# One fused attention and wave-MLP kernel, its steps written out in another order

## The chip, the core and the metric

The kernel runs on one of the eight cores of a Trainium2 chip. A core has four compute engines, each with its own queue of instructions: TensorE (PE; its weight loads are listed apart, as PEld), VectorE (DVE), ScalarE (ACT) and GpSimd (POOL). SyncE (SP) has a queue too and issues nearly all DMA transfers. The engines run side by side, and wait for each other through semaphores. The metric is the device time of one execution in microseconds (us), lower is better.

## The reference

Eight batches; in each, an attention over 8 heads of 576 tokens with 64 channels, and behind it a small token-and-channel network on 576 x 512 values. The attention is the sum of two: one over q, k and v averaged in fours (144 tokens, every output repeated four times), and one in which a token sees only the tokens less than 4 away.

```python
q_d, k_d, v_d = (t.reshape(B, H, Sd, 4, D).mean(axis=3) for t in (q, k, v))
out_up = np.repeat(sm_attn(q_d, k_d, v_d), 4, axis=2)
mask = np.abs(pos[:, None] - pos[None, :]) < 4
scores = np.where(mask, scale * q @ k^T, -1e9)
out_local = softmax(scores) @ v
x = (out_up + out_local) as [batch, token, 512]

theta = x @ w_theta
zr, zi = x * cos(theta), x * sin(theta)
y = w_tok_r @ zr + w_tok_i @ zi          # mixes tokens
u = x + y
out = u + relu(u @ w_ch)
```

Inputs and output are float32.

## The kernel before, in words

All compute runs in bfloat16 with float32 sums. The work of a batch is cut into steps of one function each, named by two letters; one step issues some instructions on one engine. The order is not left to a scheduler: the string `ORDER` names every step of the whole kernel in one row, 1,191 words, and `pin()` chains each instruction to the one before it on its engine, so every queue (SyncE's too) is in exactly the order of the words. A word is the step's two letters and a place; which batch and which part of it is meant follows from counting (the third `mx` is the third in the list of `STEPS`). The place is a PSUM bank or a pair of banks for steps on PE, a staging slot for loads, and the engine (`v`, `a`, `g` for DVE, ACT, POOL) for casts, copies and means.

The steps of a batch, in the order in which they need each other:

- `lk`, `lq`, `lv` and `lw` load k and q (four loads of 288 KB each) and v (ten of 128 KB: five windows, two halves) into one of 16 staging slots (L287, L347); v of batch 0 comes by `l1` (L365). A slot is free again when its cast has read it. `la`, `lb`, `lc` load the weights.
- `ck`, `cq`, `cv` cast to bfloat16 (L295, L396). `tp` transposes k or q on PE (L302), `ev` copies the result out of PSUM (L315); for batch 7 a DMA does it (`dk`, L306). `kd`, `qd` take the means of four (L321 on DVE, L329 to L335 on POOL).
- `ps`, `ex`, `mk`, `po`, `nm` are the local attention: scores (L482), exponential (L490), band mask (L503, L505), product with v (L515), division (L523, L524). `pv`, `vd`, `sd`, `ed`, `nd`, `xn`, `xd`, `xc` are the averaged one (L404 to L470).
- `xt` transposes the local result (L537) and `xa` adds the averaged one to it (L545): x, transposed, in `xT`.
- `th`, `cs` make theta and its cosine and sine (L556, L561, L562), `xm` transposes x back (L595), `zz` multiplies (L620, L615 for batches 6 and 7). `tt`, `ct`, `zt`, `zp`, `zc` or `dz` do the same for the last 64 tokens (L568 to L590).
- `mx` is the mixing of tokens: eight parts of nine matmuls with 288 columns (L636), each followed by `ua`, which adds x (L641). `wp`, `wc` transpose its weights once, in the beginning.
- `up`, `uc` or `du` transpose u (L650, L653, L645); `ch` projects it (L666), `rl` makes the output (L674), `st` stores it (L680). `ut`, `dt`, `ht`, `rt`, `ss`, `sr` do this for the last 64 tokens of two batches at a time (L656 to L709).
- `te` and `ts` let ACT load the table of the exponential or the sine ahead of its use (L770), and `wm` runs idle matmuls on zeros (L764). Six more idle matmuls belong to the constants (L226).

So a batch's q goes load, cast, transpose, copy, mean, and only then can its averaged scores (`sd`) start; its theta can start only when both attentions are through, its mixing only when all of its z is there. The order interleaves two or three batches, so that one batch's mixing fills PE while the next one's attention goes from engine to engine.

Of the kernel before, what the change touches and what calls it, by code (L numbers as in the profile page):

```python
# [58 lines left out]
lq8 x14 cka x15 cqg evv cva lk9 tp67 ckg cvv cva lqa lqb tp01 lk1 cqg x14 cva wm521 evv evv cqa qdv tp23 cva la3 eva
pv47 vda wm624 ps01 kdg la6 ps23 ex kdv ckg lq4 ex wm656 wm717 lq2 ps01 qdg lk5 sd67 mkv ckv cqg sd45 po23 ed lk8 cag  # L60
ed ex po67 lq9 lba nm cba nd45 nm nd23 xn cag mkg cqa tp01 po67 xn po45 nm lkb eva xd0 mkg ckg lq7 cka xca la1 po23 nm
tp67 cag xt45 la0 xt01 nm lb3 lb4 lb5 cqg lbc xa lba lb2 xt23 xa eva tp67 lb8 cqg lb1 caa ts th4 kdg cs cbg xm5 xa lv7
evv lw th0 th2 lv0 cbv lw zz cbg tt3 xm4 lv3 cs cbg cbv ct cbg cbg cs lvb lw lw wp0 wcv wp1 wcv ztg wp5 th3 wp1 lv8
wcv xm2 cbg xm0 zz zp7 tp45 cs qdg wp3 wp6 zz wcv lw zz wcv wcv zca eva wp7 wcv wp1 wca te wp0 wcv ps34 ps56 ex ex
ps12 mx0 lq1 cvg lk2 lka mx7 lqc mx3 qdv cvg ua lk7 ex ua lk0 mkv mkv kdg sd67 po45 nm sd12 lq4 cva lk5 lk9 cvg cvg ed
ed mx0 ua ua lq3 pv67 po45 po23 nm mx0 vda mkg nd67 lk8 nd45 lkb nm xn xn lq6 ckg ckg tp12 mx3 po45 ua lca ua nm cqg
cqg tp67 eva eva xd0 ckg ckg up1 lq7 po23 lvc xcv nm tp45 xt67 cqg mx0 cqg xt23 eva xt45 lv4 qdg kdg uca lw lv0 lw lw
lv3 lv1 lw lw xa xa tp67 cka ts ckg ckg th1 th2 xa th5 lk8 xm4 evv cs cqg xm1 ckv th3 zz tt4 up6 lq6 lqb cs zz tp12
xm7 ua cs ucv ct cs cqg eva te ztv xm6 zz zz mx0 ua tp34 zp7 tp56 ps12 zcv mx7 mx0 ex cvv kdg evv eva lk7 lk9 cvg lk4
qdg ua up7 uca sd12 mkv ps34 po56 ex ua ccv lcc lc5 kdg nm mkv mx0 sd34 ed po56 cvg cvg ua cqg mx7 nm ua ed mx0 ua lk2  # L70
cka cqg ps67 lqd lq0 cva po45 nm lca ex po23 ckg ckg nm pv01 lvb mx6 vda lk6 utv lw tp45 eva lv1 lw cca ccv nd01 nd23
ua xn xn qdg tp67 mx5 eva lv8 lv9 cqg cqg lw lw ccg ps34 qdg ps67 ua ps12 kdv ex ex xd0 lva xca lw mkg mkg lqc lq0 ch5
rl ckg ckg cvg cvg ch3 sd67 xt45 mkg ed rl ex ts mx0 xa xt67 po45 lv5 th1 cs xa nm ua tp23 th7 up4 up1 ucv xt56 xa mkv
lv4 ch0 eva po56 po23 cvg lq2 tt4 uca th1 cs th7 nm st nm xm2 lqb rl lq1 zz lqd ct cvg xm6 lw cqg ch5 cs zz cs cqa te
up0 up1 rl sd23 ucv po67 ch4 nm rl ch0 rl ucv tp67 lv7 ed cvg pv45 vdv lk8 lk9 eva st st tp23 eva xm0 ztg lk0 lka lw
xm1 zz zz zp7 ch6 zca lvc lv3 kdg nd45 xn nd23 ckg tp01 cva xn qdg utg mx7 cka ps23 rl kdg eva ps01 ua po45 mx6 up7 ex
ex lw lw lv8 nm qdg lw cqg po45 cqg ucv lvb lv2 lw sd23 sd01 lv5 ed mx7 lw lw ua tp23 nm xd4 ed ckg ckg xca st evv
tp01 eva mx6 mkg xt45 xt23 ua ua cva cvg cvg xt01 cka ts cvg xa xa mx7 th6 xa po45 nm pv23 tt0 th1 lk4 xm4 st st mkg
th5 vdv st cs nd23 ua zz ct cqg cqg ztg tp67 th4 cs dt po01 cs cs te xn evv po23 mx5 kdg qdg xm4 xm6 mx7 nm ps01 ex nm
ps23 ua lvd ua ex ch5 ps01 ex qdg zz lw lw xm7 zz rl kdg zp6 zz mkg nd23 xn lv1 lva lv3 mx5 zca sd67 lw ps01 ex po34  # L80
mx2 ua lw ed tp01 sd67 cva nm po34 eva cvv cvg ed lw up5 uca ua mx2 cvg nm cvg lvc xd3 ua pv04 xcv lk7 lk0 mx7 lq9 lq6
lq2 lqd lq8 lqb lq5 ckg ckg vda lq7 lw xt56 mkv cqg cqg po34 lk4 xt01 xa xa ch2 st cva ts lv6 th5 up6 ckg xm0 nm th1
tp34 cs ucv cs mkg rl eva mx6 ua ua th1 xt67 lk0 lk1 cs cqa po45 mkv xa nm ht3 rt tp67 th1 eva zz xm2 lv9 xm3 xm4 lw
lve zz zz ckg dk4 kdv mx0 cqg tp67 nd23 xn cs zz ua cqa eva mx1 nd67 xn cqa sr cqa cka tt2 ct dkb up4 cva cva ua mx0
mx7 ua cvg cvv uca te po01 nm qdg kdg qdg sd56 ed po23 ua ch4 rl xd0 ch1 ztg lw nm up7 ch4 uca xca po23 dz xt67 rl evg
ckg nm st st pv15 vda mx0 ps23 xa ex rl up1 up7 evg ua ucv mx6 uca ss ps01 ex xt45 cqa utg xa ua lv1 dk4 ps23 ex mx7
up0 uca th4 lvb sd56 mkv po23 lw lw xt01 utg dt ua dk7 cvv nm th7 du ed ts evg nd56 xa nd23 tt0 xn xn ct qdg mkv mkg
evv mx1 ztg xd2 up0 ua cs ch3 rl cs te mx4 ch7 qdg ps56 rl xcv ua mx1 ex cvg po23 po45 ua uca ps67 ex ht1 nm nm st st
rt cva ss mx0 ua po67 xt45 nm ps23 st xa ex ts du kdg th1 xm0 xm7 cs th6 cs xm4 zz zz zz ch5 rl kdg mx7 ua th0 po67 nm
cs te xt45 xa sd12 ch3 xm0 ch7 ch4 xt56 st ed sd12 mkg mkg ed ts zz dz lw mx0 lv1 du du cvv lw cvg th1 cs rl uta mx3  # L90
st rl rl xa dxb ua po45 po67 pv02 nm nm ua du mx1 vda ch4 dx mkg ua po23 po01 po67 rl sr nm mx5 ua mx4 tt5 dx1 du nm
nm nd23 xn nd01 st mx6 th7 mx2 cs xn xd3 mx0 ua ua xcv ua ua xt67 utv ct dx st st xt45 xt23 xa ch1 rl th0 ch6 ch1 ch7
cs xa xa tt0 zz zz th2 th3 cs st du du ch4 rl zz zz ztg ct dz rl mx2 mx0 mx1 cs ua ua st dxe dx ht0 ua th1 cs th3 dx7
dx zz st st mx2 rl mx1 ua ua cs zz dt mx3 mx1 mx2 zz zz ztg dz mx7 ua mx3 du du du mx6 rt ua ua utg ua st rl du st mx7
mx4 ua ua ua sr mx7 mx6 mx5 ua ua ua du du ua ch7 ch6 ss ch5 rl rl ch7 ch6 ch4 ch3 du du st uta dt sta rl st rl ht7
ch2 sta rl st rl sta rl st rt ssa sr rl sta rm su k0
"""


# [450 lines left out]


# [256 lines left out]
```

## Time and profile before

| | us |
|---|---|
| median of 3 runs | 231.89 |
| lowest, highest run | 229.57, 232.5 |
| span of the profiled execution | 232.2 |
| PE busy in it | 217.7 |
| DVE busy | 187.7 |
| ACT busy | 156.2 |
| POOL busy | 145.0 |

The profiled execution is one of its own beside the timed runs; of its time the profile has the span, from the first to the last instruction, and no other figure. A matmul's end is modelled in the profile and matmuls overlap, so a busy PE is not PE at its peak. The chain of waits is followed back from the last instruction: at each piece to what released it.

### The profile page before, as it was taken

To read this page: it belongs to the slowest core of one execution; us is meant where nothing else is said; L and a number is where in the kernel's file an instruction comes from. 1 tells how busy PE (TensorE), PEld (TensorE's weight loads), DVE (VectorE), ACT (ScalarE), POOL (GpSimd) and SP (SyncE) were. 2 spreads that over 40 slices of the span, in tenths; PEclk is the share of its full clock that TensorE was granted. 3 is DMA by queue.
4 is the path that set the end of the run, shared out by engine and by line. 5 is a ranking of instruction groups with operands and counts; after the bars stand their busy time and mean duration, and the time that the engine had idled before them with its cause. 6 is when DMAs were issued, how large, how long until landed. Compare 5 with 4: busy or idle time off the path is not lost.

```text
span 232.2 us, 9404 instructions
## 1 busy us (share of the span) xinstructions
PE 217.7 (94%) x3943; PEld 152.6 (66%) x3970; DVE 187.7 (81%) x367; ACT 156.2 (67%) x243; POOL 145.0 (62%) x192
## 2 busy tenths in 40 slices
PE   7997899999999999899999989989998999999992
PEld 3655678877877666776775675756655775668741
DVE  5699888999988799789968887698986978558473
ACT  4589799689988898898877978778788232430000
POOL 7689977879985999879963489598952001100000
PEclk9999799999999999999999999999999999999999
DMA  6999968997999689968999996892284358656587
GB/s 217 395 390 390 291 114 238 361 300 118 265 391 179 165 245 285 243 142 214 205 165 347 307 213 115 206 153 92 67 149 109 71 127 193 138 159 137 142 227 245
DMA packets 76795, 49.41 MB, mean 213 GB/s; under 512 B 61136, under 2 KB 61392, under 8 KB 76752
## 3 DMA queue, kind: packets, MB, share of 16 engines
q1 hardware_dynamic: 76096, 47.76, 81.9%
q10 hardware_dynamic: 656, 1.05, 1.3%
q8 instruction: 31, 0.51, 0.9%
q14 instruction: 12, 0.10, 0.1%
HBM read 33.98 MB, written 9.44 MB: 187 GB/s over the span
## 4 chain that ended last, share of the span: by engine, by line
PE 60%; DMA 10%; POOL 10%; issue 6%; ACT 5%; DVE 4%; SPq 4%; DVEq 0%; POOLq 0%; ACTq 0%
PE PS L636 21%; PE PS L666 9%; PE PS L556 8%; DMA st<-in_q_dram 6%; PE PS L302 4%; POOL two L329 3%; PE PS L515 2%; SPq L347 2%; DMA st<-in_k_dram 2%; PE PS L537 2%; DMA ur<-uT 2%; POOL q_tm L295 2%; PE PS L482 2%; PE PS L447 1%; PE PS L595 1%
## 5 line engine op out<-in xcount | busy, mean ns | idle before, releaser
L636 PE MATMUL PS<-WT,z 128*128 128x288 bf16 x576 | 78.0, 287 | 0.0
L636 PEld LDWEIGHTS <-z 128*128 128x128 bf16 x576 | 53.9, 98 | 15.9 <-issue 1.3
L641 DVE TENSOR_TENSOR uT<-PS,xT 128x288 bf16<-128x288 f32 x64 | 28.6, 452 | 12.7 <-PE PS L636 10.9
L561 ACT ACTIVATE cs<-PS,pihc 128x512 bf16<-128x512 f32 x32 | 22.0, 689 | 21.1 <-PE PS L556 13.4
L556 PE MATMUL PS<-wth,xT 128*128 128x512 bf16 x116 | 30.8, 383 | 0.7 <-issue 0.2
L666 PE MATMUL PS<-wch,uT 128*128 128x512 bf16 (+1 forms) x122 | 29.8, 373 | 0.9 <-issue 0.6
L524 DVE TENSOR_TENSOR tmp<-PS,rl 128x512 bf16<-128x512 f32 x40 | 27.7, 692 | 1.4
L545 DVE TENSOR_TENSOR xT<-PS,xdT 128x928 bf16<-128x928 f32 (+1 forms) x24 | 22.3, 952 | 3.7 <-PE PS L537 2.3
L674 DVE SCALAR_TENSOR_TENSOR osb<-PS,ur 128x512 f32<-128x512 f32 x28 | 19.1, 687 | 7.1 <-DMA ur<-uT 3.0
L490 ACT ACTIVATE pm<-PS 128x1024 bf16<-128x1024 f32 (+1 forms) x24 | 20.5, 880 | 6.2 <-PE PS L482 6.1
L577 POOL TENSOR_TENSOR zT<-xT,cst 128x512 bf16<-128x512 bf16 x7 | 9.7, 1383 | 20.6 <-ACT cst L574 20.6
L295 POOL CAST k_tm<-st 128x576 bf16<-128x576 f32 x23 | 15.1, 668 | 11.2 <-DMA st<-in_k_dram 11.1
L396 POOL CAST v_w<-st 128x512 bf16<-128x512 f32 x21 | 13.3, 651 | 10.6 <-DMA st<-in_v_dram 10.5
L770 ACT ACT_TABLE_LOAD x15 | 19.2, 1283 | 0.3
L666 PEld LDWEIGHTS <-uT 128*128 128x128 bf16 x132 | 11.9, 98 | 11.2
L562 ACT ACTIVATE cs<-PS 128x512 bf16<-128x512 f32 x32 | 19.1, 597 | 0.0
L556 PEld LDWEIGHTS <-xT 128*128 128x128 bf16 x128 | 11.7, 99 | 10.6 <-issue 0.6
L295 POOL CAST q_tm<-st 128x576 bf16<-128x576 f32 x23 | 15.4, 686 | 4.9 <-DMA st<-in_q_dram 4.7
L503 POOL TENSOR_TENSOR pm<-pm,band 128x512 bf16<-128x512 bf16 x16 | 18.3, 1164 | 0.0
L329 POOL TENSOR_TENSOR two<-qT 128x576 f32<-128x576 bf16 x14 | 16.5, 1177 | 0.7 <-ACT qT L315 0.4
L620 DVE TENSOR_TENSOR z<-PS,cs 128x1024 bf16<-128x1024 bf16 x24 | 15.8, 684 | 0.5 <-ACT cs L562 0.3
L437 ACT ACTIVATE pd<-PS 128x864 bf16<-128x864 f32 x16 | 13.8, 889 | 2.5 <-PE PS L426 2.5
(124 smaller groups left out, 422.9 us busy)
## 6 DMA issues: line engine op xcount, KB each, us to landing
st<-in_k_dram SPq DMA_DIRECT2D x32, 288.0 KB, 6.5
st<-in_q_dram SPq DMA_DIRECT2D x32, 288.0 KB, 6.3
...
```

Of the source, the lines that this page charges most:

```text
L295: COPY[w](out=to, in_=of)
L329: nc.gpsimd.tensor_tensor(out=t, in0=src[:, :, 0:2], in1=src[:, :, 2:4], op=ALU.add)
L490: nc.scalar.activation(out=pm[(3 * b + u) % NPM][:, :, 0:n].rearrange("p e c j w -> p e (c j w)"), in_=at.pop(("ps", b, u))[:, :, 0:4 * W ...
L524: nc.vector.tensor_tensor(out=tmp[(NCH * b + c) % NTMP].rearrange("p g (j d) -> p g j d", d=D), in0=ps[:, :, :, 0:D], in1=r.unsqueeze(3).t ...
L545: nc.vector.tensor_tensor(out=xT[b % 2][:, :, lo:lo + cnt].rearrange("p e (m j) -> p e m j", j=4), in0=at.pop(("xt", b, u))[:, :, 0:cnt].r ...
L556: nc.tensor.matmul(out=ps, lhsT=xT[b % 2][:, dc, P * c:P * c + P], rhs=wth[:, dc, :], start=(dc == 0), stop=(dc == 3))
L561: nc.scalar.activation(out=t[:, 0, :], in_=ps, func=AF.Sin, bias=pihc, scale=1.0)
L562: nc.scalar.activation(out=t[:, 1, :], in_=ps, func=AF.Sin, bias=0.0, scale=1.0)
L636: nc.tensor.matmul(out=ps, lhsT=z[b % 2][:, j, P * dc:P * dc + P], rhs=WT[:, j, cols], start=(j == 0), stop=(j == 8))
L641: nc.vector.tensor_tensor(out=uT[b % 2][:, dc, cols], in0=at.pop(("mx", b, i)), in1=xT[b % 2][:, dc, cols], op=ALU.add)
L666: nc.tensor.matmul(out=ps[:, cols], lhsT=uT[b % 2][:, dc, P * c:P * c + P], rhs=wch[:, dc, cols], start=(dc == 0), stop=(dc == 3))
L770: nc.scalar.activation(out=idle, in_=pihc, func=TABLE[kind])
```

## The change

Two things change. The first is `ORDER`: the same steps in a new row, again 1,191 words, with other banks, other slots and in part other engines. Nine more casts of k and q go to DVE (11 rather than 2), four fewer to ACT (12 rather than 16) and five fewer to POOL (41 rather than 46); three more of the `zt` go to DVE. The idle matmuls of `wm` are 25 with 10,560 columns, where they were 32 with 15,424. Table loads stay 16. The second is the code of `xt` and `xa`: the pair of banks may now be two that do not lie next to each other. What is multiplied and added, and with how many columns, stays.

```diff
 ORDER = """
-kcg l10 l11 l12 l13 kcv lk4 lq5 c1a wm7e0 kcg c1g t101 lk6 lk7 ckg c1a ckg c1v t123 e1a kcv e1v wm737 tp01 x12 cqa x13
...
+l10 lk1 ckv lk2 l13 c1a cka kcg c1v l14 l15 lq6 lq7 cqg lk0 wm087 tp01 t123 lk8 lq1 c1a evv kdv kcv c1a ckv cqg e1a
...
     def xt(b, u, w):
-        ps = at["xt", b, u] = pair(w).rearrange("p k (x n) -> p (k x) n", x=2)
+        ps = at["xt", b, u] = pair(w).rearrange("p k (x n) -> p k x n", x=2)
...
-                        nc.tensor.matmul(out=ps[W * (j % 2):W * (j % 2) + W, 2 * hf + j // 2,
+                        nc.tensor.matmul(out=ps[W * (j % 2):W * (j % 2) + W, hf, j // 2,
...
         nc.vector.tensor_tensor(
-            out=xT[b % 2][:, :, lo:lo + cnt].rearrange("p e (m j) -> p e m j", j=4),
-            in0=at.pop(("xt", b, u))[:, :, 0:cnt].rearrange("p e (m j) -> p e m j", j=4),
-            in1=xdT[b % 2][:, :, lo // 4:(lo + cnt) // 4].unsqueeze(3).to_broadcast([P, 4, cnt // 4, 4]),
+            out=xT[b % 2][:, :, lo:lo + cnt].rearrange("p (k x) (m j) -> p k x m j", k=2, j=4),
+            in0=at.pop(("xt", b, u))[:, :, :, 0:cnt].rearrange("p k x (m j) -> p k x m j", j=4),
+            in1=xdT[b % 2][:, :, lo // 4:(lo + cnt) // 4].rearrange("p (k x) m -> p k x m", k=2).unsqueeze(4)
+            .to_broadcast([P, 2, 2, cnt // 4, 4]),
             op=ALU.add)
```

The code grows by one line, so lines from L549 on are one higher in the changed kernel.

SyncE's queue around the loads of batch 6, before: the thirteen loads of v are of batches 4 and 5, the ten of batches 5 and 6, and the eight of q are batches 6 and 7. `st` is the staging area, `osb` an output buffer, `utr` the transposed last tokens.

```order
L347 DMA st_126<-in_v_dram 64x8x64 x13
L680 DMA out_0_dram<-osb3_121 128x512
L287 DMA st_126<-in_k_dram 128x576
L680 DMA out_0_dram<-osb4_122 128x512
L680 DMA out_0_dram<-osb0_118 128x512
L680 DMA out_0_dram<-osb1_119 128x512
L695 DMA_TRANSPOSE utr_117<-ut0_115 128x4x128
L347 DMA st_126<-in_v_dram 64x8x64 x10
L287 DMA st_126<-in_k_dram 128x576 x2
L287 DMA st_126<-in_q_dram 128x576 x8
```

And now: the seven loads of v are of batches 4 and 5, the four of q behind them are batch 6, the fifth is batch 7's first, and the three of k are batch 6.

```order
L347 DMA st_126<-in_v_dram 64x8x64 x7
L287 DMA st_126<-in_q_dram 128x576
L347 DMA st_126<-in_v_dram 64x8x64
L287 DMA st_126<-in_q_dram 128x576
L347 DMA st_126<-in_v_dram 64x8x64
L287 DMA st_126<-in_q_dram 128x576
L347 DMA st_126<-in_v_dram 64x8x64
L287 DMA st_126<-in_q_dram 128x576
L347 DMA st_126<-in_v_dram 64x8x64
L287 DMA st_126<-in_q_dram 128x576
L287 DMA st_126<-in_k_dram 128x576 x3
```

The q of batch 6 has moved ahead of sixteen loads of v and between the others; ahead of its first load there were 57 loads of v and 82 other issues, and there are now 41 and 71.

VectorE's queue in the start, behind the constants, before. `k_tm` and `q_tm` are casts of k and q, `kT` and `qT` their transposes, `kd` and `qd` the means, `z0` here holds v of batch 0, `pm` the exponentials.

```order
L371 CAST z0_103<-st_126 128x8x64
L371 CAST z0_103<-st_126 128x64
L231 COPY band_131<-full0_135 64x64 x2
L379 COPY xT1_102<-PS_61 128x1152
L315 COPY kT0_62<-PS_61 128x2x576
L393 CAST v_w0_70<-PS_61 128x8x64
L315 COPY qT0_64<-PS_61 128x1152
L315 COPY kT0_62<-PS_61 128x2x576
L321 TENSOR_REDUCE qd0_68<-qT0_64 128x288
L321 TENSOR_REDUCE kd0_66<-kT0_62 128x2x5x29
L505 TENSOR_TENSOR pm0_83<-pm0_83,band_131 128x1024
L295 CAST k_tm2_76<-st_126 128x9x64
```

And now:

```order
L295 CAST k_tm0_74<-st_126 128x9x64
L371 CAST z0_103<-st_126 128x8x64
L371 CAST z0_103<-st_126 128x64
L315 COPY kT0_62<-PS_61 128x2x576
L321 TENSOR_REDUCE kd0_66<-kT0_62 128x2x5x29
L231 COPY pu1_133<-full2_137 64x32 x2
L295 CAST k_tm1_75<-st_126 128x9x64 x2
L315 COPY kT0_62<-PS_61 128x2x576
L231 COPY band_131<-full0_135 64x64 x2
L295 CAST q_tm2_79<-st_126 128x9x64
L321 TENSOR_REDUCE qd0_68<-qT0_64 128x288
L393 CAST v_w0_70<-PS_61 128x8x64
```

Four casts of k and q stand there now where one stood, and the copies out of PSUM for q and for v's first transpose have gone to another engine.

More of the change, by code (lines that the diff above doesn't have):

```diff
@@ L57 @@
 ORDER = """
-kcg l10 l11 l12 l13 kcv lk4 lq5 c1a wm7e0 kcg c1g t101 lk6 lk7 ckg c1a ckg c1v t123 e1a kcv e1v wm737 tp01 x12 cqa x13
[L59 to L96, printed above, removed]
+l10 lk1 ckv lk2 l13 c1a cka kcg c1v l14 l15 lq6 lq7 cqg lk0 wm087 tp01 t123 lk8 lq1 c1a evv kdv kcv c1a ckv cqg e1a
@@ new lines @@
+wm422 t101 lq2 ckv cqg e1a wm431 tp23 x14 x15 tp01 eva x12 cqg cva kcg qdg lk9 lq3 x14 cva cva lk4 lk5 lq6 lk7 la0 lb8
+la1 la2 evv kcv cqv lba tp67 eva cva la3 lbb lbc wm341 ps01 x16 ex qdv cvv ps45 ckg kdg wm311 pv01 ckg ex ckg cqg cbg
+cag mkv vda cag sd45 po67 lb9 mkv po23 sd01 lq4 ed ed nm nm po67 lq5 lb6 tp45 lb0 nm eva nd23 xn lb1 ps01 nd67 xn tp45
+xt23 ex po01 eva xd6 xca nm lb8 xa cag cba lv2 ckg mkg wm711 xt45 po01 cbg cbg caa tp67 nm xa eva cbg th2 lw lv3 lw
+lv9 xt01 cqg wp3 wp6 cqg cbg lv6 lw kdg cbg cbg wcv cs wp7 wcv xa th4 wcv cbg tp56 tt0 xm7 ts cs lw lv8 xm1 wp2 th3
@@ new lines @@
+evv zz ct xm0 zz th7 xm1 cs ztv wcv lw zp6 wp3 cs ts wca zz wp2 wp5 wp0 ps47 zcv wcv zz wcv lk1 lk0 ps26 qdg ex wcv
+lq5 wp3 wcv kdv mx1 mx3 ua qdg cvg lq2 sd45 ex lk4 lqc lka ps07 ua mkv cvg mx1 ed ex po45 cva ua sd23 po67 nm nm cva
+mkg mx0 ed po45 cvg ckg mkg pv12 ckg cqg po67 te vda mx3 nd12 nm nd45 nm ua ua xn mx3 tp01 xn cqg xd2 ua xca eva po45
+xt67 cka nm mx3 xa tp45 xt01 xt67 th2 xa lv8 lq6 eva ua cs ckg cqg lq9 lk1 lk3 lk0 lw lv2 lq4 lva up4 xm5 lw tp01 ucv
+xa evv th3 lw lvc lk5 lcb lq7 tt4 cqg qdg ckg lv1 lw lw cqg cs ct tp67 xm2 th0 ztg ckg th3 cs zz evv mx6 xm7 up0 cs zz
@@ new lines @@
+zp1 kdv tp23 xm4 zca eva zz ua zz cqv kdg ps57 mx6 ex mx1 tp23 cvg eva ckv ua cvv qdg mx6 cvg mkv ckg sd45 utv ua ps23
+po17 ua mx6 ed lq2 lka ex lq5 lc0 lk8 lc4 lc3 kdg cvg ccv nm po45 sd17 cqa ed cvg tp23 ckg ucv ua nm mkv mx6 eva ua
+pv01 po45 lv7 lq1 po23 lw vda cqv lk2 lva lw up6 lkc lvb mx7 lv9 lq6 lvd lke lw ucv nm up6 nd01 lw nm tp45 uca eva xn
+ua mx6 ps01 ps23 lw ua ps45 nd67 ex ex qdv kdg ccg ckg ccg cqg ccg up0 ex uca xn mkg ch1 tp23 rl qdg xd4 xt67 ps01 mx5
+eva xcv cva xa po23 xt67 ex sd01 nm mkg ua xa ch4 cqa ed cka te cvg tp23 up5 th0 lqa eva mkg kdg cqg ckg cvg rl ucv st
@@ new lines @@
+po67 po14 xt23 lq2 lk1 lq7 cs nm xa nm th5 ch6 tt7 xm4 cs up1 ct xm0 th2 rl zz ucv zz ch3 xm0 tp67 cs th2 cvv rl ckg
+qdg zz cqg cva ztg eva po01 sd45 pv36 nm ckg lk3 lv5 lkc ch7 cs vdv rl lw st lvd lq1 ed lw ch2 xm3 zp6 tp01 lqa lve
+zca eva zz rl tp45 nd67 nd23 mx0 eva xn xn uta po45 kdg mkg qdg ps67 nm cqg mx1 po45 sd23 cqa ex ckg ed kdg ua cvg
+ps67 ua nm ch0 up1 xd2 ckv mx3 ex sd67 uca rl xcv xt01 xa ua cva xt45 ed cqa cqa mx2 ts tp01 lv7 lv9 lw mkg lw mkg cvg
+lw th3 eva lv5 lqd lv1 lqa tp67 cvg lvc lq3 lw lq7 lw xa ua lqe evv lk2 lkb tp45 lk6 st st th2 mx0 st lk4 cvg cs lv9
@@ new lines @@
+evv ua cs pv67 xt45 po01 xm2 th3 dt lv8 xa nm lw vda po67 lw lv0 po45 xm0 th1 cs cqg zz tt3 nm nd67 cs mx2 xm1 nm qdg
+qdg ps45 xn zz ua zz ps67 ct ztg kdg cvg nd03 te ex xn mx2 po45 ps01 ex ex ckg cqg cvg mkv ckg cqg mkg ckg mkg ps67 ex
+nm ua mx3 sd01 ed po45 sd67 nm ch2 xm0 zp1 xd4 zz zcv ua mx5 xt01 ua ed xca xa xt67 xa xt34 mx5 th0 up1 tp67 cs uca lw
+lk3 lw rl xa evv lv6 ch2 xm3 th4 tp67 cva cvg xm1 eva mx0 ckv ua rl xm2 tp67 ua zz cqv cs mx0 tt3 up4 eva ct cvg mkg
+kdg qdg zz ua lqb lk1 lw lv4 po67 pv15 mx3 lvc vda nm tp67 lw lk7 cqa lq8 ztv ucv ua lw st lk9 nd45 th3 nd01 lva st
@@ new lines @@
+lve xn cka eva dz lw ts cs mx4 up5 ht3 th6 ua kdg xn mx4 cs cva cqg qdg cvg te ckg zz ucv po01 sd25 ps67 ed te uta ex
+dk1 lq0 cvv cvg ckg rt evg mkg ua nm ckv xd3 ch4 xm0 ch1 mx2 rl zz po45 ps67 ua rl nm mx0 xca po23 ex sd67 xt45 ua cva
+ed cqa nm xa ch1 up0 pv23 uca po67 ps45 st dk7 st st ss mx0 nm lw te th6 mx7 vda rl ua ua ex cqa evg dk1 sr dk0 lv7
+xt01 xt45 po23 xa nm xa mx7 th0 up1 ts cs xm6 xm4 tt5 nd23 zz uca th6 cs cvg eva ct utv ua zz xn up7 mx0 up1 nd45 mkg
+qdg ucv eva cs qdg mkg ua xn ucv mx0 po23 ps67 ps45 ua nm xd1 mx0 ex ex ch2 mx3 mkv xca rl ua te xt45 po67 ua nm xa
@@ new lines @@
+po12 th0 lw lve cs mkv uta kdg ztg kdg cvg xm3 ht6 xm7 lv8 th4 du st ch5 lw dt st rt lw dz du zz nm up6 ch3 st sr cvg
+lve lw ss ch2 rl zz rl cva po01 uca cs xt45 ps67 mx3 nm xa ts ex ua mx0 po67 xt45 sd13 rl nm xa ua du du dx8 dx st du
+dx7 dx mx2 mkg st po67 cvg ed sd45 po13 ua nm ed th0 mx2 mx6 ua cs nm tt7 pv23 po01 po45 ct vda nm nm mx7 nd23 ch0 xn
+ztv rl zz ua st nd45 dz mx2 th3 ch0 ua th1 cs xn ua xd2 xca cs mx3 ch2 rl zz ua zz zz xt45 xt01 xt67 mx3 rl xa ua mx2
+ch3 utg ua ch4 xa xa rl mx5 th6 st cs th3 du dt du dx7 dx ht2 du dx8 mx6 dx tt7 th0 mx1 st du cs st ua cs ua ua ct ztv
@@ L97 @@
+zz zz mx3 rl ua th7 ch6 ts cs ch1 ch7 mx3 mx0 dz du zz ua st zz rl rl mx3 du st ua rl ua mx6 ua mx0 k0 mx3 ua rt mx0
+mx2 ua mx3 mx1 ua ch0 ua ch2 ch6 ua ua ch1 st du st rl du du ss sr rl du st du ch0 ch7 st rl utg ch6 sta utg ht2 dt st
+ch3 rl rl rl rl sta rt st sta st ts rm rl ssa sr su sta
 """
```

## The prediction

> **What bounds the kernel now.** I read the page's busy shares first, then cut the span into stretches, then followed the chain of waits through the stretch that looked worst, then the sync queue there.
>
> ```profile
> span 232.2 us, 9404 instructions
> PE 217.7 (94%) x3943; PEld 152.6 (66%) x3970; DVE 187.7 (81%) x367; ACT 156.2 (67%) x243; POOL 145.0 (62%) x192
> ...
> PEclk9999799999999999999999999999999999999999
> ...
> q1 hardware_dynamic: 76096, 47.76, 81.9%
> ```
>
> TensorE is busy for 94% of the span, so the order can win only what PE waits, 14.5 us in all. Two other things are nearly full as well: VectorE (81%) and the DMA engines (81.9%), and the DMA share is an average over a kernel whose loads lie in its first two thirds. The next view gives busy time by stretch (PE, PEld, DVE, ACT, POOL, then granted clock, DMA share, GB/s).
>
> ```profile
> core 0: us, PE busy (x) PEld busy (x) DVE busy (x) ACT busy (x) POOL busy (x), PEclk, DMA share, GB/s
> ...
> 12.00:37.00 25.00, 22.20 (x557) 16.74 (x562) 23.33 (x40) 22.08 (x35) 22.55 (x30) 0.93 0.92 284
> 37.00:115.00 78.00, 76.69 (x1620) 56.35 (x1628) 69.49 (x132) 66.65 (x100) 67.37 (x86) 1.00 0.95 242
> 115.00:161.00 46.00, 43.05 (x822) 30.70 (x826) 37.70 (x72) 36.76 (x59) 32.54 (x34) 1.00 1.01 205
> 161.00:205.00 44.00, 42.65 (x700) 27.61 (x707) 33.44 (x66) 21.86 (x40) 13.97 (x15) 1.00 0.53 116
> 205.00:228.00 23.00, 22.86 (x160) 15.54 (x159) 15.55 (x29) 2.62 (x5) 0.40 (x1) 1.00 0.69 188
> 228.00:232.20 4.20, 0.00 (x0) 0.00 (x0) 0.71 (x2) 0.00 (x0) 0.00 (x0) 1.00 0.62 195
> ```
>
> PE's idle time is 2.80 us in 12 to 37, 1.31 in 37 to 115, 2.95 in 115 to 161, 1.35 in 161 to 205, 0.14 in 205 to 228, and 4.2 after its last matmul. The stretch 115 to 161 stands out: PE idles 6.4% of it against 1.7% of the stretch before, while the DMA engines are at 1.01 and VectorE, ScalarE and GpSimd are all less busy than before it. The chain of waits says why (start, length, what):
>
> ```profile
> 113.24 0.61 ACT pm L490
> 113.85 0.54 SPq L347
> ...
> 117.72 1.75 SPq L347
> 119.51 0.73 SPq L287
> ...
> 121.08 4.99 DMA st<-in_q_dram
> ...
> 126.13 0.67 POOL q_tm L295
> ...
> 130.37 3.81 issue
> ...
> 134.81 0.67 POOL q_tm L295
> ...
> 141.16 0.68 POOL qd L335
> ```
>
> From 113 to 142 it holds almost no PE work: SyncE issues loads of v one after another (L347), then at 121.08 the first q loads of batch 6 (L287), which land 5 us later; GpSimd casts them, waits again, casts the last at 134.81 and takes the means up to 141.8. The queue itself:
>
> ```profile
> 92.95 12.75 SPq L347 DMA_DIRECT2D st<-in_v_dram  x13
> ...
> 108.34 2.02 SPq L695 DMA_TRANSPOSE utr<-ut  x1
> 110.46 9.01 SPq L347 DMA_DIRECT2D st<-in_v_dram  x10
> 119.51 1.20 SPq L287 DMA_DIRECT2D st<-in_k_dram  x2
> 121.08 4.92 SPq L287 DMA_DIRECT2D st<-in_q_dram  x8
> ```
>
> A load of v (half a chunk, rows of 256 bytes) takes 0.90 to 0.98 us of the queue, and 23 of them stand between 92.95 and 119.5. A load of q takes 0.62 (4.92 / 8). So batch 6 came late because it was queued behind v, and not because its slots were taken: SyncE goes from one issue to the next.
>
> **The change part by part.** Both orders hold the same steps; some casts, evictions and means change engines. The ends are alike too: from the last mixing matmuls of batch 6 on, the same eight of batch 7, eight projections and the last stores follow in the same sequence, so the 23 us to 228 and the 4.2 us of tail stay (0).
>
> *Loads of batch 6 (gain 2.6).* Ahead of its first q load stood 57 loads of v and 82 other issues; now it is 41 and 71. Sixteen loads of v at 0.90 are 14 us of queue, the eleven others at 0.6 nearly 7. The request can go out near 121.08 - 21 = 100, and PE wants its product only at 135. What PE lost in its absence:
>
> ```profile
> PE PS L302 <- POOL q_tm L295: 0.8, 1, 0.8
> PE PS L426 <- POOL qd L335: 0.3, 1, 0.3
> PE PS L515 <- DVE pm L505: 0.8, 1, 0.8
> ```
>
> The first two are surely this chain, 1.1 us. Had the stretch idled like the one before (1.7% of 46 is 0.77), it would have saved 2.95 - 0.77 = 2.2. The upper end comes from weight loads: 30.70 of 46 us here, 56.35 of 78 (72%) before; at 72% the same loads need 42.5 us, 3.5 fewer. The lower end is 0, if the wait only moves. I take 2.6, near the row of idle time since that is seen directly. [...]
>
> *The start (0, from -2.8 to +3.4).* The first twelve loads are batch 0's in both, so its scores cannot come sooner. After that k and q of batch 1 are asked for ahead of the weights. Ahead of the last weight cast GpSimd has a mask and a zT fewer and two casts more; ahead of the last z of batch 0 VectorE has three steps more, ScalarE two evictions more and four casts fewer. Gains and losses of one or two instructions stand against each other, so I take 0. All PE idle of 12 to 37 is 2.8, which is the most that can go; the loss is bounded under the next part.
>
> *Idle matmuls (0 of the start's range).* Their row and the clock's cost:
>
> ```profile
> L764 PE MATMUL PS<-warm 128*128 128x512 bf16 (+4 forms) x30 | 7.4, 379 | 0.2 <-issue 0.2
> PE PS L466 <- ACT kT L315: 0.7, 1, 0.7
> 13.60:17.10 3.50, 3.34 (x87) 1.98 (x87) 3.47 (x4) 3.11 (x6) 2.98 (x5) 1.00 1.06 392
> 17.10:20.50 3.40, 2.44 (x88) 1.70 (x87) 3.33 (x7) 3.40 (x6) 3.40 (x5) 1.00 1.05 391
> 20.50:23.90 3.40, 2.27 (x67) 1.93 (x64) 3.26 (x9) 3.23 (x5) 3.40 (x5) 1.00 1.06 371
> 23.90:27.30 3.40, 3.17 (x112) 2.97 (x114) 2.79 (x5) 2.30 (x4) 3.32 (x6) 0.65 1.05 298
> ```
>
> From 15,424 columns to 10,560 is 2.3 us of 7.4. They stand where PE would wait anyway, so removing them is worth nothing by itself. But PE's clock fell once, near 24 us, after two stretches of 3.4 us in which PE was busy only 72% and 67%. One such dip takes at most 25 x 0.07 = 1.75 us. Each further dip is another 1.7; two of them are the +3.4. [...]
>
> *Engines (0).* Nine more casts of k and q stand on VectorE ahead of the last z of batch 4, three more evictions, two fewer masks:
>
> ```profile
> L295 DVE CAST k_tm<-st 128x576 bf16<-128x576 f32 x2 | 1.5, 742 | 0.0
> L641 DVE TENSOR_TENSOR uT<-PS,xT 128x288 bf16<-128x288 f32 x64 | 28.6, 452 | 12.7 <-PE PS L636 10.9 <-ACT cs L562 0.8 <-ACT kT L315 0.4
> L505 DVE TENSOR_TENSOR pm<-pm,band 128x1024 bf16<-128x1024 bf16 (+1 forms) x10 | 8.9, 902 | 0.0
> 137.60 0.68 DVE L620 TENSOR_TENSOR z<-PS,cs 128x1024 bf16<-128x1024 bf16 x1
> 146.39 1.21 PE PS L636 x9
> ```
>
> 9 x 0.742 + 3 x 0.452 - 2 x 0.902 = 6.2 us; the rest are single instructions that cancel. The z was ready at 138.3 and used at 146.4, so 8.1 us of cover hide the 6.2 and leave 1.9. The cover is gone if PE also arrives earlier: its order brings it there some 1.6 us of matmuls sooner, and by the 2.6 above.
>
> *Banks and the rest (gain 0.6, from -3 to +1.4).* New banks re-deal every short wait. PE idles 1.31 + 1.35 = 2.7 us in the two other long stretches, which bounds the gain; the loss I bound by the worst stretch's idle time, 2.95. I take a quarter of the gain, as with nothing to tell one bank from another a re-deal is near even.
>
> The sum: 2.6 + 0 + 0 + 0.6 = 3.2 us. The profiled span, 232.2, lies 0.3 above the median of the runs and inside their range; against the median, 231.89 - 3.2 = **228.7 us**, 1.4% less.
>
> **The rivals.** *PE gets denser everywhere.* The same eased queue and the shuffled banks take away all idle of 37 to 205 (5.6 us) and the 2.8 of the start: 223.5. For it: each wait is below 1 us, so little slack is needed. Against it: VectorE is 89% busy in 37 to 115 (69.49 of 78).
>
> *The loads were not the pace, and the gain is eaten.* VectorE's z of batch 4, with 1.9 us of cover against 1.6 + 2.6 us of earlier arrival, is late by 2.3 us, and the time is 231.89 - (2.6 + 0.6 - 2.3) = 231.0, up to 232 if the q loads wait for their slots instead. This is also the case that the change does not do what it says.
>
> *Slower: the clock.* The place is 8 to 30 us. Between the first transposes and the end of the scores of batch 0 stood 6,272 idle columns (3.0 us of the row above), now 2,688 (1.3). Without 1.7 us the stretch before 17.1, nearly full until now, is busy about half. If PE at two thirds or less costs the clock for the next 3.4 us, three stretches follow, 5.1 us, and no gain outlives it as what comes late is PE's own work: 231.89 + 5.1 = 237.0. It decides when three stretches fall below 67%. Against it: much of PE's work there waits for ScalarE (22.08 of 25 us) and would not feel a slower clock in full.
>
> **How the numbers follow.** The forecast 0.45, from 225.6 (3.5 + 2.8 us gained) to 230.8 (only the two sure waits, 1.1); denser PE 0.28, near 223.5; eaten gain 0.11, at 231 to 232.5; clock 0.16, at 236.5 to 239. Two per cent, about what a measurement here tells from no change, is 4.6 us: faster is below 227.3, slower above 236.5. The forecast's low quarter and the dense case make faster 0.40 (0.12 + 0.28); the rest of the forecast and the eaten gain 0.44; the clock 0.16. Leaving out the clock and the lowest 0.04 gives the range 222 to 235.
>
> **What would show it.** Right: q of batch 6 issued near 100 to 110, GpSimd without a wait like the 3.81 us in the chain above, PE idle in the stretch around batch 5's mixing near 1.7%. The start: the granted clock of the page's first eight slices, and when the first mixing matmul begins:
>
> ```profile
> 36.89 1.28 PE L636 MATMUL PS<-WT,z 128*128 128x288 bf16 x9
> ```
>
> Eaten: matmuls of batch 4 that wait for L620 or L621. Wrong altogether: a new chain through loads of v for batch 4, whose second halves now follow at once on a slot that a cast of batch 5 frees.

## The result, and the profile after

The changed kernel is slower: 248.95 us, the median of 4 runs (246.35 to 250.86), where the kernel before had 231.92 beside it. The ratio is 1.069, with a 95% interval from 1.058 to 1.079. The prediction was 228.7 us, from 222 to 235. Executions that lie over 1.5% above the fastest of their kernel are left out of the ratios, here and below, though not out of the medians, so where the two differ the ratio decides.

The page of the changed kernel (the profiled execution took 246.35 us):

```profile
span 244.6 us, 9373 instructions
PE 219.0 (90%) x3934; PEld 153.8 (63%) x3963; DVE 187.5 (77%) x366; ACT 159.5 (65%) x245; POOL 140.9 (58%) x190
...
PEclk9999999999979999999999997999999999999997
```

TensorE is busy as long as before (219.0 us against 217.7), and so is VectorE; what has grown is the time in which TensorE does nothing, 25.6 us where it was 14.5. Besides the last slice, in which TensorE hardly works, two have a lower clock (0.7 in the page), near 70 and 150 us, and neither lies in the start. The stretches say where TensorE idles. After:

```profile
core 0: us, PE busy (x) PEld busy (x) DVE busy (x) ACT busy (x) POOL busy (x), PEclk, DMA share, GB/s
37.00:60.00 23.00, 21.16 (x412) 16.33 (x412) 20.20 (x36) 17.76 (x28) 15.31 (x21) 1.00 0.81 237
60.00:75.00 15.00, 11.30 (x225) 8.17 (x222) 10.21 (x21) 9.23 (x11) 9.39 (x13) 0.89 0.82 205
115.00:145.00 30.00, 28.27 (x526) 21.12 (x528) 22.86 (x45) 21.15 (x35) 23.85 (x30) 1.00 1.01 228
145.00:157.00 12.00, 8.80 (x214) 6.00 (x212) 6.93 (x16) 7.52 (x13) 7.71 (x7) 0.86 0.99 189
```

And the same stretches of the kernel before:

```profile
37.00:60.00 23.00, 22.95 (x449) 17.68 (x450) 20.84 (x40) 19.40 (x30) 19.03 (x26) 1.00 0.93 256
60.00:75.00 15.00, 14.91 (x349) 11.55 (x347) 13.24 (x29) 13.14 (x20) 11.39 (x15) 1.00 1.09 298
115.00:145.00 30.00, 28.04 (x490) 20.11 (x491) 24.04 (x49) 24.38 (x39) 20.33 (x24) 1.00 1.10 228
145.00:157.00 12.00, 11.07 (x301) 7.88 (x301) 10.18 (x19) 8.40 (x15) 9.02 (x9) 1.00 1.00 174
```

In 60 to 75 us all four compute engines are less busy than before, and the DMA engines too. No engine is the bound there: they wait for each other. The instructions of that stretch in order of time (start, length, what; in brackets the idle time ahead of it and what ended it):

```profile
62.48 1.02 ACT L490 ACTIVATE pm<-PS 128x1024 bf16<-128x1024 f32 x1
...
63.53 0.46 DVE L642 TENSOR_TENSOR uT<-PS,xT 128x288 bf16<-128x288 f32 x1 [1.23 <-ACT pm L490]
...
64.04 1.26 PE L637 MATMUL PS<-WT,z 128*128 128x288 bf16 x9 [0.66 <-DVE uT L642]
...
67.16 1.26 PE L637 MATMUL PS<-WT,z 128*128 128x288 bf16 x9
...
68.53 0.21 DVE L523 RECIPROCAL rl<-PS 128x8 f32<-128x8 f32 x1 [0.85 <-PE PS L637]
...
69.51 0.32 PE L515 MATMUL PS<-v_w,pm 64*64 64x65 bf16 x16 [1.09 <-DVE tmp L524]
...
70.08 0.89 ACT L437 ACTIVATE pd<-PS 128x864 bf16<-128x864 f32 x1 [2.04 <-PE PS L426]
...
71.00 0.46 DVE L642 TENSOR_TENSOR uT<-PS,xT 128x288 bf16<-128x288 f32 x1 [1.21 <-ACT pd L437]
71.02 1.12 PE L302 MATMUL PS<-ident,k_tm 128*128 128x128 bf16 x9 [0.99 <-ACT pd L437]
```

These releasers make no sense by the data. The addition `ua` (L642, 63.53) adds x to a mixing product of batch 1; it needs nothing of the exponential of batch 2's scores (L490), yet it waits 1.23 us for it. The reciprocal at 68.53 belongs to a product with v that was done before 67.16, and waits until the mixing matmuls behind it are done. The transposes of k at 71.02 wait for an exponential of other scores. The largest single wait is of the same kind (at 146 us; L705 is `rt`, the output of leftover tokens, and L437 the exponential of batch 6's averaged scores):

```profile
146.11 0.36 PE L426 MATMUL PS<-qd,kd 64*64 64x144 bf16 x12
...
148.06 0.87 ACT L437 ACTIVATE pd<-PS 128x864 bf16<-128x864 f32 x1
148.97 0.69 DVE L705 SCALAR_TENSOR_TENSOR osb<-PS,utr 128x512 f32<-128x512 f32 x1 [3.13 <-ACT pd L437]
...
149.71 0.64 PE L466 MATMUL PS<-ident,xdn 72*128 72x72 bf16 x8 [2.98 <-DVE osb L705]
```

What these places share stands in the words. The scores at 62.48 lie in `ps57`, on banks 5 and 7; the addition that waits reads bank 6. The reciprocal's product is `po17`, on banks 1 and 7, and the mixing product it waits for is again on bank 6. The transposes wait behind `sd17`. At 146 us the scores are `sd25`, `rt` reads bank 3, and the matmuls that wait (`xd3`) write it. The changed order puts eleven such products on a pair of banks that are not neighbours, each of which one instruction reads. The kernel before has none: the only split pairs in its order are `pv`, which is read bank by bank.

The program's own semaphores say the same. VectorE's queue in the changed kernel, the addition of batch 1 with what it waits for:

```
103 L642 TENSOR_TENSOR uT1_112<-PS_61,xT1_102 128x288 [waits Activation_49]
```

It does not name TensorE, which writes its operand; the exponential waits for that mixing product, and the addition for the exponential.

### The profile page after: what moved, and what is told of

Read it like the earlier page. It is cut to its first block, busy times and chain, and to the rows that moved or that the text cites. A ratio compares the mean times of both kernels' runs of the same rounds, so it can differ in the third digit from the quotient of the medians.

```text
span 244.6 us, 9373 instructions
## 1 busy us (share of the span) xinstructions
PE 219.0 (90%) x3934; PEld 153.8 (63%) x3963; DVE 187.5 (77%) x366; ACT 159.5 (65%) x245; POOL 140.9 (58%) x190
## 5 line engine op out<-in xcount | busy, mean ns | idle before, releaser
L637 PE MATMUL PS<-WT,z 128*128 128x288 bf16 x576 | 79.8, 289 | 1.9 <-DVE xdn L458 1.1
L637 PEld LDWEIGHTS <-z 128*128 128x128 bf16 x576 | 54.6, 99 | 18.3 <-issue 2.5
L642 DVE TENSOR_TENSOR uT<-PS,xT 128x288 bf16<-128x288 f32 x64 | 28.4, 450 | 23.0 <-PE PS L637 17.4
L667 PE MATMUL PS<-wch,uT 128*128 128x512 bf16 (+1 forms) x121 | 31.0, 381 | 1.0 <-issue 0.5
L657 POOL COPY ut<-uT 128x256 bf16<-128x256 bf16 x3 | 1.6, 532 | 42.6 <-DVE uT L642 42.6
L490 ACT ACTIVATE pm<-PS 128x1024 bf16<-128x1024 f32 (+1 forms) x24 | 20.5, 880 | 6.9 <-PE PS L482 6.2
L503 POOL TENSOR_TENSOR pm<-pm,band 128x512 bf16<-128x512 bf16 x18 | 20.8, 1179 | 3.0 <-ACT pm L490 3.0
L667 PEld LDWEIGHTS <-uT 128*128 128x128 bf16 x132 | 12.6, 100 | 12.9 <-issue 1.4
L437 ACT ACTIVATE pd<-PS 128x864 bf16<-128x864 f32 x16 | 13.9, 888 | 6.6 <-PE PS L426 3.5
L329 POOL TENSOR_TENSOR two<-kT 128x580 f32<-128x580 bf16 x13 | 15.0, 1151 | 4.6 <-ACT kT L315 3.8
L515 PE MATMUL PS<-v_w,pm 64*64 64x65 bf16 x640 | 11.6, 195 | 5.6 <-DVE tmp L524 2.4
L295 POOL CAST q_tm<-st 128x576 bf16<-128x576 f32 x20 | 13.3, 675 | 5.2 <-DMA st<-in_q_dram 5.1
L515 PEld LDWEIGHTS <-pm 64*64 64x64 bf16 x640 | 8.3, 107 | 12.5 <-issue 6.1
```

Source lines behind the costliest of these rows:

```text
L329: nc.gpsimd.tensor_tensor(out=t, in0=src[:, :, 0:2], in1=src[:, :, 2:4], op=ALU.add)
L490: nc.scalar.activation(out=pm[(3 * b + u) % NPM][:, :, 0:n].rearrange("p e c j w -> p e (c j w)"), in_=at.pop(("ps", b, u))[:, :, 0:4 * W ...
L503: EW[w].tensor_tensor(out=t[:, x], in0=t[:, x], in1=m[:, x], op=ALU.mult)
L515: nc.tensor.matmul(out=ps[W * hf:W * hf + W, g, j, :], lhsT=t[W * g:W * g + W, e, i, blk, :], rhs=v_w[b % 2][W * g:W * g + W, c, 4 * hf + ...
L637: nc.tensor.matmul(out=ps, lhsT=z[b % 2][:, j, P * dc:P * dc + P], rhs=WT[:, j, cols], start=(j == 0), stop=(j == 8))
L642: nc.vector.tensor_tensor(out=uT[b % 2][:, dc, cols], in0=at.pop(("mx", b, i)), in1=xT[b % 2][:, dc, cols], op=ALU.add)
```

## The experiments

Theory A: an instruction that reads two banks with others between them counts, where the waits are put in, as one that touches the whole stretch from the lower to the upper. It waits for work on the banks between, and work there waits for it. Rival B: eleven of the sixteen table loads of ScalarE (1.28 us each) now come in line, at the first exponential or sine. Rival C: the longer queue of VectorE and the new engines of casts. Rival D, later: banks that really are held too long by the new order.

**Neighbouring banks.** 22 bank numbers differ, for the eleven split pairs (the expectation says twelve), of which these are three:

```diff
-ps57
+ps45
-po17
+po01
-sd25
+sd45
```

> The changed kernel, with 22 bank numbers altered and nothing else: the twelve steps that the change put on two banks that are not neighbours (four, five and seven and the like) get neighbouring banks. Theory A (the tracker of dependencies takes such a pair as the whole stretch of banks from the lower to the upper, so that a step on a bank in between waits for work it does not need): the TensorE idle stretches of 1.57 us at 42 us, 0.66, 0.91, 1.09 and 1.00 us between 62 and 71 us, 1.09 us at 120 us and 2.98 us at 147 us go, 9.3 us in all, and with the two stretches of low clock behind them (1.7 us each) up to 12.7 us: 236 to 241 us. Rival B (the exponential's and the sine's tables are loaded at the first use, in line, 11 times 1.28 us): no change, 247 to 250 us. Rival C (longer queues on VectorE or the new engines of casts): no change, 247 to 250 us.

Measured: 244.26 us (241.34 to 245.72), ratio 1.057 [1.047, 1.066]. By the medians 4.7 us came back, by the ratios 1.2 points (some 2.8 us) with intervals that overlap; either is less than theory A had. The waits listed above are gone from its trace, but the new numbers brought others. Of TensorE's two largest, the first has no releaser (more of this at the end); in the second a projection now takes the bank that batch 6's averaged scores hold:

```profile
PE PS L482 <- issue: 2.0, 1, 2.0
PE PS L667 <- ACT pd L437: 1.9, 1, 1.9
```

So this run moved two things, the pairs and who takes which bank when.

**Table loads.** 15 words `te` and `ts` moved ahead of the first uses.

> The changed kernel with its 15 table-loading words moved: each stands behind the last use of the other table, at the longest gap of ScalarE before the first use, as in the kernel before. Theory A (banks): no change, 247 to 250 us. Rival B (loads in line): up to 11 x 1.28 = 14 us less of ScalarE in front of TensorE's waits, 236 to 245 us.

Measured: 247.63 us (245.43 to 249.19), ratio 1.072 [1.063, 1.082]. TensorE's largest waits in its trace are as long as the changed kernel's (3.0, 2.4 and 1.9 us). Rival B falls: where the tables are loaded does not matter here.

> Both edits together. Theory A: as with the neighbouring banks alone, 236 to 241 us, within 1 us of that run. Rival B: as with the table words alone. If both hold, lower than either by over 2 us.

Measured: 246.03 us (239.58 to 247.4), with no interval. Three of the four runs took 245.9 us or more, above the run with neighbouring banks, and one took 239.58; this run settles nothing.

**Split pairs in the kernel before.** Its own order, with nine of its steps on the split pairs of the changed kernel, and the 18 other numbers that this forces.

> The kernel before, with its own order, engines, loads and table words, and 27 bank numbers altered: nine steps get the split pairs that the change gives to the same steps (for batch 1 the three window stages; the first window stage, its output and the second part of the dense scores of batch 2; one step each of batches 3, 4 and 6). Theory A: 3 to 9 us slower than before, 235 to 241 us. Rivals B and C: as before, 230.5 to 233.5 us.

Measured: 242.55 us (240.56 to 243.21), ratio 1.052 [1.045, 1.060]: 12 us slower, more than theory A had said, with nothing of the new order in it. But 18 other numbers had moved too.

**The same banks, read one at a time.** The next runs keep every word of the order and only issue the eviction of a split pair twice, so that no instruction spans the banks between:

```diff
-        nc.scalar.activation(out=pm[...], in_=at.pop(("ps", b, u))[:, :, 0:4 * W * n], func=AF.Exp, scale=SCL)
+        ps = at.pop(("ps", b, u))[:, :, 0:4 * W * n]
+        for s in parts("ex", b, u):      # (0:1, 1:2) for the split pairs, (0:2) for all others
+            nc.scalar.activation(out=pm[...][:, s], in_=ps[:, s], func=AF.Exp, scale=SCL)
```

and likewise in `ed`, `nm` and `xn`. Line numbers rise by up to 14. All eleven:

> The changed kernel with its own order and its own banks, word for word; only the eleven evictions that read a pair of banks that are not neighbours are issued twice, once for each bank, so that no instruction spans the banks in between (11 instructions more on ScalarE and VectorE and as many short reciprocals, some 0.2 us each by the price of a second instruction of that size). Theory A (waits for work on the banks in between): the seven idle stretches of TensorE whose releaser has nothing to do with the waiting step go: 1.57, 0.66, 1.09, 0.99, 1.09 and 2.98 us, 8.4 us, and one or both stretches of low clock (1.7 us each), less 1 us for the added instructions: 236 to 241 us. Rival D (the order itself: banks really held too long by steps that VectorE and ScalarE reach late, which the run with neighbouring banks showed at other places, 0.5 to 1.9 us each): 242 to 247 us.

Measured: 239.6 us (237.32 to 241.74), ratio 1.034 [1.025, 1.043]; repeated below, 240.07 us, 1.036 [1.031, 1.041]. By the medians 9.4 of the 17.0 us are back, by the ratios 3.5 of 6.9 points, some 8 us: about half, by an edit that adds instructions. Its page and what it does at the place shown above (now L501, L656 and L535 for L490, L642 and L523):

```profile
span 235.6 us, 9428 instructions
PE 218.6 (93%) x3963; PEld 152.5 (65%) x3963; DVE 188.1 (80%) x374; ACT 160.0 (68%) x252; POOL 141.5 (60%) x190
...
PEclk9999999999999999999999999999999999999999
```

```profile
60.71 0.45 DVE L656 TENSOR_TENSOR uT<-PS,xT 128x288 bf16<-128x288 f32 x1
60.97 1.08 ACT L501 ACTIVATE pm<-PS 128x512 bf16<-128x512 f32 x2
...
65.66 0.24 DVE L535 RECIPROCAL rl<-PS 128x4 f32<-128x4 f32 x2
```

The addition now runs before the exponential that it had waited for, and the semaphores that it waits for are TensorE's and VectorE's own:

```
103 L656 TENSOR_TENSOR uT1_112<-PS_61,xT1_102 128x288 [waits DVE_49,PE_49]
```

Only batch 2's three, and only batch 6's one:

> As the run before, but only for the three evictions of batch 2 (the first window stage, its output, the second part of the dense scores). Theory A: the idle stretches of 0.66, 1.09 and 0.99 us between 63 and 71 us go, and perhaps the 0.91 us between them and the low clock behind them (1.7 us): 2.7 to 5.3 us less than the changed kernel, 243 to 246 us. Rival D: less than 1.5 us, above 247 us.

Measured: 247.82 us (244.28 to 250.6), ratio 1.062 [1.051, 1.074]. By the median this is 1.1 us less than the changed kernel, in rival D's range; by the ratio 0.7 points (some 1.5 us), and the interval holds both theories. Not clear. In its trace the three waits are gone, but TensorE then stands without any wait, as it does in other runs (see the end), and the granted clock behind it is 0.68 from 80 to 84 us:

```profile
78.47 0.35 PE L491 MATMUL PS<-qT,kT 64*64 64x64 bf16 x18 [2.17 <-issue]
```

> As the run before, but only for one eviction: the first part of the dense scores of batch 6, on banks two and five. Theory A: the idle stretch of 2.98 us at 147 us goes, and with it the low clock behind it (1.7 us): 3 to 4.7 us less than the changed kernel, 244 to 246 us. Rival D: the next step of TensorE waits there instead, less than 1.5 us, above 247 us.

Measured: 245.17 us (243.04 to 246.74), ratio 1.064 [1.055, 1.072], inside theory A's range by its median, though the intervals overlap. The trace is plainer than the time. The stretch around the wait, changed kernel first, then this one:

```profile
146.00:150.00 4.00, 1.02 (x67) 1.00 (x67) 1.03 (x3) 3.97 (x8) 1.20 (x2) 0.92 1.04 238
150.00:152.00 2.00, 1.78 (x11) 0.90 (x10) 1.49 (x4) 0.88 (x2) 2.00 (x2) 0.50 0.99 254
```

```profile
146.00:150.00 4.00, 4.00 (x90) 2.71 (x89) 3.97 (x10) 3.38 (x6) 1.82 (x4) 1.00 1.25 126
150.00:152.00 2.00, 2.00 (x31) 1.22 (x29) 1.22 (x3) 2.00 (x6) 1.27 (x1) 1.00 1.01 292
```

One eviction issued twice takes the 2.98 us away and the half-rate clock behind it.

**The price of the second reads.** The kernel before, with the same eleven evictions in two:

> The kernel before, with the same eleven evictions issued once for each bank; its pairs are all neighbours, so this is the price of the added instructions alone. All theories: 0 to 1.5 us more than the kernel before, 230.5 to 233.5 us. Below that, or more than 2 us above it, and the gain of the run with the changed order cannot be read as the waits alone.

Measured: 231.52 us (229.25 to 237.36), ratio 1.002 [0.997, 1.007]. The additional instructions cost nothing that can be measured, so what the edit gives back elsewhere is waits.

**The same edit where only the banks were changed.** The split pairs in the kernel before (242.55 us), their evictions in two:

> The kernel before with the 27 bank numbers that gave it nine split pairs (242.55 us, where the kernel before had 230.54), and the evictions of these pairs issued once for each bank. Theory A (an eviction that spans two banks waits for, and holds back, whatever works on the banks between): most of the 12 us goes, 231 to 235 us. Rival H (the 27 new numbers themselves cost it, because banks are taken again too soon): 239 to 243 us.

Measured: 233.7 us (232.93 to 235.12), ratio 1.016 [1.009, 1.022]. Of the 12 us that the split pairs and the 18 other numbers had cost, 8.9 were waits for banks in between; the numbers themselves cost about 3. Before and after the edit, TensorE:

```profile
PE 219.3 (91%) x3943; PEld 153.2 (64%) x3970; DVE 187.5 (78%) x367; ACT 156.4 (65%) x243; POOL 145.7 (61%) x192
```

```profile
span 231.2 us, 9444 instructions
PE 219.2 (95%) x3970; PEld 152.2 (66%) x3970; DVE 186.4 (81%) x375; ACT 156.9 (68%) x250; POOL 146.8 (63%) x192
```

The same work, in a span of 240.2 and of 231.2 us. In both orders the edit gives back about 3.5 points of the ratio (1.069 to 1.034 and 1.052 to 1.016), though it changes neither the order nor a bank. Theory A holds, for about half of the loss.

**What is left.** The changed kernel with its reads in two is still 8 us slower than the kernel before. Its trace has two waits of the order (1.07 us near 64 us, 1.25 us near 164 us), and two stretches near 74 and 80 us (1.16 and 1.95 us) in which TensorE stands and no semaphore is late (at the second the profile names VectorE's addition, but that had ended 0.5 us before TensorE went on).

> The kernel whose eleven evictions read in two, with two places of the changed order mended: on VectorE the second addition of batch 1 goes ahead of the mask of batch 2 that it stood behind (TensorE waited 1.07 us at 63.6 us for its bank), and four bank numbers near 163 us let the first window stage of batch 7 start without a bank that ScalarE's sine still reads (1.25 us). Theory D (the rest of the loss is such places of the order): 2 us less, 237 to 238 us where that run had 239.6. Rival: the next late step stands right behind, less than 1 us, 238.6 to 240.6 us.

Measured: 239.07 us (237.16 to 240.65), ratio 1.040 [1.030, 1.050]. No gain; the next waits (0.85 us at 65, 1.00 at 169) stand where the two were.

> The kernel whose eleven evictions read in two, with one thing changed: the ten loads of v for batch 3 read rows of 2 KB instead of rows of 256 bytes, as many bytes from other places (so batch 3 is computed from other elements of v). Theory F (what is left over the kernel before is partly TensorE's instructions coming late: in that run it stood 1.16 us at 74.0 and 1.95 us at 80.0 without any wait, and started again 1.5 us after a block of 16 KB of instructions had landed, 1.46 and 1.71 us in transfer beside the loads of v, 0.9 to 1.1 elsewhere): both stretches go or halve, 1.5 to 3.1 us less, 236.5 to 238.1 us where the run before had 239.6. Rival G (those two stretches have another cause, the order of the steps): no change, 238.6 to 240.6 us.

Measured: 241.18 us (238.44 to 243.39), ratio 1.040 [1.030, 1.049]. No gain in time. In the trace the first stretch is gone and the second is 0.57 us, but TensorE stands 1.33 us in the same way at 123 us, and the mean granted clock of that execution is 0.990, where the first with reads in two had 0.998.

> The changed kernel with its eleven evictions in two, and with 3,584 more idle columns ahead of 17 us (three words longer), as many as the kernel before has there. If the clock at the start costs the changed kernel time (the rival of the prediction): 1.5 to 5 us less than the run without them, 234.5 to 238 us. If not: 239 to 241.5 us, the idle columns themselves costing up to 1.7 us.

Measured: 241.64 us (238.77 to 246.3), ratio 1.040 [1.031, 1.049]. Giving the idle matmuls of the start back won nothing.

> The changed kernel with its eleven evictions in two, once more, to compare the next two with: 238 to 241 us by every theory.

> That kernel with the waits of the order taken away together with those that took their place in the run with two places mended: the second addition of batch 1 ahead of the mask of batch 2, the copy of the leftover tokens behind the third addition, and five bank numbers near 165 us. Theory D: 2 to 2.5 us less than the repeated run (1.07 us at 64 us and 1.25 us at 164 us). Theory F: within 1 us of it.

> The same, and the loads of v for batch 3 in rows of 2 KB (other elements of v for that batch). Theory F: 2 to 3 us less than the run with the steps moved (the stretches near 74 and 80 us). Theory D alone: within 1 us of it. Both: 4 to 5.5 us less than the repeated run, about 235 us; what is then left over the kernel before lies in no single place.

Measured, on one chip: 240.07 us (239.02 to 244.57), 244.23 (242.52 to 245.63) and 240.63 (238.66 to 243.52); ratios 1.036 [1.031, 1.041], 1.054 [1.049, 1.059], 1.034 [1.028, 1.041]. Mending these places of the order made it 4 us slower, not 2 us faster. Theory D's form, that the rest is a few places which can be mended one by one, falls. The trace of the middle run shows a new wait of 2.07 us at 172 us, for the division that empties a bank, and a longer stretch without a wait:

```profile
73.81 0.72 PE L500 MATMUL PS<-qT,kT 64*64 64x64 bf16 x62
77.17 0.48 PE L500 MATMUL PS<-qT,kT 64*64 64x64 bf16 x18 [2.64 <-issue]
```

The long rows took 3.6 us off it by the medians and 2.0 points (4.6 us) by the ratios, more than theory F had said, which leads back only to the repeated run and not to 235 us; and the trace still has such a stretch at the same instruction (2.36 us), so it does not say that this is how. How far TensorE stands behind its own work, by the place in its work (the start of a step in the trace, less the matmul time of the steps ahead of it, each at its usual length; us), shows where the 8 us lie, in one execution of each kernel:

```
work done   before, reads in two   changed, reads in two   changed
 18                17.8                    18.5              18.3
 42                20.0                    20.4              22.8
 66                22.6                    27.6              29.7
108                26.0                    31.4              35.1
126                27.6                    33.2              41.1
138                28.6                    36.1              43.9
186                31.0                    38.4              47.0
```

Both orders with reads in two lose alike except between 42 and 66 us of work (2.6 and 7.2) and between 126 and 138 (1.0 and 2.9). In these two places lie the scores of batches 2 and 3 and those of batch 7. In that execution the idle stretches named above make up most of the difference: 1.07, 1.16 and 1.95 us in the first place, 1.25 us in the second. But the profiled execution of the repeated run (240.69 us, where the first took 237.32) has no stretch at 80 us and only 0.36 us near 76; in it the clock was low in the start instead (18 to 30 us, a granted clock of 0.72):

```profile
18.00:30.00 12.00, 9.22 (x248) 7.84 (x250) 9.28 (x18) 8.42 (x13) 10.93 (x17) 0.72 1.00 315
```

So the rest does not always sit in the same place, and what it is was not settled.

## Why the prediction was wrong

The step that failed is "Banks and the rest (gain 0.6, from -3 to +1.4)", and in it the sentence that there was "nothing to tell one bank from another". There was: eleven evictions on split pairs, which cost some 8 us by the ratios (9.4 by the medians), nearly three times the bound of 3. That is about half of the loss. The other half, some 8 us, also falls under "the rest" of this term; the runs speak against table loads and idle matmuls as its cause, and what it is stays open. The bound was taken from the idle time of the worst stretch before, and no row of a kernel without split pairs can show their price. But the diff hints at it: `xt` and `xa` were rewritten so that a pair need not be neighbours. (None of the eleven is an `xt`; they are `ps`, `sd`, `po` and `nd`, whose code took such pairs before.) The words show which pairs are split, and the waits of the built program show what they wait for; the prediction read the order for sequence and engines, not for waits. The wait of VectorE's addition for ScalarE, on the queue quoted above, could have been read before any run.

- *Loads of batch 6 (gain 2.6).* They moved as foretold. SyncE's queue in the changed kernel, the requests for q of batch 6 from 97 us on:

```profile
97.42 0.61 SPq L287 DMA_DIRECT2D st<-in_q_dram  x1
98.08 7.47 SPq L347 DMA_DIRECT2D st<-in_v_dram  x7
105.64 0.69 SPq L287 DMA_DIRECT2D st<-in_q_dram  x1
...
109.69 0.61 SPq L287 DMA_DIRECT2D st<-in_q_dram  x1
```

The gain was not there to be had. TensorE's 1.96 us of idle time in 115 to 145 belonged to that one execution. In the kernel before with reads in two the same stretch has no wait for q of batch 6 at all, and in the changed kernel with reads in two it is full:

```profile
115.00:145.00 30.00, 29.63 (x573) 21.24 (x574) 25.72 (x52) 25.52 (x44) 21.80 (x26) 1.00 1.00 236
```

```profile
115.00:145.00 30.00, 30.00 (x583) 22.10 (x582) 24.98 (x52) 23.34 (x39) 24.48 (x31) 1.00 1.13 232
```

In that execution the loads could give at most 0.37 us there, and 0.58 us (46 - 45.42) in the whole stretch of 115 to 161, where the prediction had counted 2.95. The term was sized from waits of a single execution, which another does not show.
- *The start (0)* and *idle matmuls (0).* Right in the profiled execution: mixing begins at 36.66 us, where it began at 36.89, and the idle columns given back won nothing. Luck has a part in it: of the twelve traces with the changed start, nine have a granted clock of 0.86 or 0.72 from 18 to 30 us, and their mixing begins at 37.54 to 39.08; the kernel before has 0.86 there in one trace and, with reads in two, 1.00 in the other. So the rival "slower: the clock" named a real place, of 1 to 2 us in some executions (an estimate from these starts) and not its 5.1; the run with the idle columns given back has 1.00 there and was no faster. In the profiled execution the clock fell at 70 and 150 us, behind the waits, and not at 8 to 30.
- *Engines (0).* No matmul of batch 4 waited for its z. The engines were not tried by themselves, so a share of the 8 us may be theirs.
- *Ends (0).* Nearly right: from 138 to 186 us of work the two orders lose alike (2.4 and 2.3 in the table above), but from the last matmul to the end of the span it is 5.4 us where it was 4.3.
- *The clock's price, 1.7 us a dip.* Two dips behind the waits, by that price (an estimate of the prediction) about 3.4 us:

```profile
66.00:70.00 4.00, 2.07 (x53) 1.46 (x53) 2.91 (x7) 2.03 (x3) 2.06 (x4) 1.00 0.89 269
70.00:72.00 2.00, 1.00 (x14) 1.03 (x11) 0.97 (x3) 0.89 (x1) 0.00 (x0) 0.71 0.95 309
72.00:74.00 2.00, 2.00 (x11) 1.15 (x8) 0.89 (x2) 1.12 (x1) 0.56 (x1) 0.50 1.11 286
```

Both are gone in both traces of the kernel with its reads in two, though the second of these has the dip in the start shown above. The dip at 150 us (0.50) lies behind a single idle stretch of 2.98 us. Ahead of the one at 70 (0.71, then 0.50) TensorE was busy 2.07 of 4 us, and no wait was over 1.1. What makes the clock fall is not shown.
